# Fewer TensorE instructions ahead of W1, and the work behind W1 put in a new order

## The chip, the cores and the metric

The kernel runs on one core of one Trainium2 chip. The metric is the device time of one execution in microseconds (us). Every kernel is compared with the kernel before in alternating rounds on the same chip.

The engines are named as in the profile: PE is TensorE's matmuls, PEld its weight loads, DVE is VectorE, ACT is ScalarE, POOL is GpSimd. A query of the profile gives lines of the form "start us, busy us, engine, source line, operation, output<-inputs, shapes, xcount", and at the end in brackets how long the engine had been idle and what released it. L-numbers are lines of the kernel at hand, so the same line of code can have another number in another version. x0, x1 and x2 are the tokens of blocks 0, 1 and 2. A warm-up is a matmul on zeros whose result nobody uses. "W1 stage" stands for what begins when the first half of the weight W1 has landed.

## The reference

Eight blocks of tokens `x` (8 heads, 512 tokens, 64 wide) attend to a small state of 32 rows and the state attends to the tokens. The result goes through a max-of-two feed-forward layer.

```python
scores = scale * x @ state^T;  a = softmax(scores);   xread = a @ state
scores2 = scale * state @ x^T; a2 = softmax(scores2); sread = a2 @ x
y = concat([xread, sread])              # per block 512 + 32 rows, 8*64 = 512 wide
out = max(y @ w1, y @ w2) @ w_out       # w1, w2: 512x1024, w_out: 1024x512
```

The kernel writes max(h1, h2) as h2 + relu(h1-h2). It therefore needs W1-W2, and the product W2·Wo, which it computes once at the start. It multiplies the small states with these matrices first ("sw") and then only multiplies by the softmax weights.

## The kernel before

The parts that matter are the order of the loads, the subtraction, the state read and the program of the first block.

```python
# loads, all in one queue, in this order
load_states(first); load_x(0, 2)
for ch in range(2):
    load_w(w2f, moe_w2, ch); load_wo(2 * ch); load_wo(2 * ch + 1)
load_w(w1f, moe_w1, 0, 2)      # first half of W1, in two pieces
load_w(w1f, moe_w1, 1)         # second half of W1
load_x(1); load_states(second); load_x(2)

def states(bs):                # transpose states on TensorE, two copies on VectorE
    ...
def w_sub(q, eng=nc.gpsimd):   # a quarter of W1 - W2
    eng.tensor_sub(wcat[:, :, cs], w1f[:, :, cs], w2f[:, :, cs])
def u_sr(b):                   # state read: 32 small matmuls, then two steps on VectorE
    ...
def l1(b, fill, fs):           # per f: two matmuls, then a relu on ScalarE or VectorE
    ...

# block 0 (cut)
w_t(0, 0, "A"); w_t(0, 1, "A")          # W2's first half transposed
u_sr(0)
...
for i in range(4): w_wo(0, i)           # W2·Wo, quarter 0
u_at(0, "V"); w_cast(w2b, w2f, 1)
for i in range(4): w_wo(1, i)
w_t(1, 0, "V"); w_t(1, 1, "A")          # W2's second half transposed
negate_states(); wo_cast(2, "P"); wo_cast(3, "P"); u_srt(0); warm_up(2)
for i in range(4): w_wo(2, i)
...                                     # W1's first half cast to bf16
for i in range(4): w_wo(3, i)
...
u_sw(0, 0); u_sw(0, 2); w_sub(0); w_sub(1)
l1(0, {}, range(0, 4))
w_sub(2, nc.vector); w_sub(3, nc.vector)
compact_x(1, 0); compact_x(1, 1); d_xt(1)   # x1 cast, then transposed by a DMA
...
l2_add(0, 0, range(0, 4)); l2_add(0, 1, range(0, 4))
states(second)
l2_add(0, 2, range(0, 4)); u_sw(0, 1); l2_add(0, 3, range(0, 4))
l1(0, {}, range(4, 8))
u_sw(1, 0)
u_exp(1, 0); u_exp(1, 1)                # block 1's scores
```

The softmax here doesn't subtract the row's maximum and nothing guards it: scores larger than these inputs give would overflow.

## Time and profile before

| | before |
|---|---|
| time, median of 6 runs | 149.94 us (149.54 to 150.0, and one stray run at 186.29, which the median counts and no comparison uses) |
| span of the profiled run | 147.9 us |
| PE busy | 139.4 us, 94% |
| W1 stage starts (first product with W1) | 22.25 us |
| first product that needs W1's second half | 30.53 us |
| layer 1 of block 1 starts | 40.01 us |

TensorE is busy 94% of the span. Of the 8.5 us of idle time, 3.4 lie in the first 22 us, where the DMA engines are full, and as much after 120 us, in the tail.

One moment serves as a yardstick: the start of layer 1 of block 1. In the kernel before and in the changed kernel the span ends 107.9 us after it, so whatever a version wins or loses is won or lost by then.

```profile
40.01 2.33 PE L308 MATMUL ps<-aT,swt 128*128 128x512 bf16 x10
```

### The profile page before, as it was taken

What the parts mean: (1) busy time and instruction counts of PE and PEld (TensorE: products, weight loads), DVE (VectorE), ACT (ScalarE), POOL (GpSimd) and SP (SyncE); (2) the same over time, 40 slices, a digit from 0 to 9 for tenths busy, and PEclk for the clock granted to TensorE, in tenths of its full rate; (3) what the DMA queues carried; (4) which work ended last, traced back from release to release, by engine and by line L of the source; (5) the groups of instructions that cost most, each with busy time, mean ns of one, the idle gap of its engine ahead of it and who ended that gap; (6) DMA issues with size and microseconds to landing.
All of it is one profiled execution on the core that took longest, in us unless ns stands there. A gap on an engine that the chain in (4) does not pass through costs nothing.

```text
span 147.9 us, 3003 instructions
## 1 busy us (share of the span) xinstructions
PE 139.4 (94%) x1228; PEld 67.4 (46%) x1249; DVE 81.7 (55%) x150; ACT 75.7 (51%) x127; POOL 44.2 (30%) x48
## 2 busy tenths in 40 slices
PE   6979899999999999999999999999999999999991
PEld 2445433434454345434443454454445434764460
DVE  5448728758887187545836581668067635721130
ACT  3175538577576268446834691477167036521011
POOL 3144269551967310640072037004100500000000
PEclk9999999999999999999999999999999999999999
DMA  4999999879999939793979497760556031502423
GB/s 75 379 387 387 387 385 340 269 138 231 262 230 307 303 68 297 273 195 118 285 226 178 177 280 188 139 284 2 106 111 284 0 75 58 226 0 70 141 89 131
DMA packets 37982, 29.89 MB, mean 202 GB/s; under 512 B 24912, under 2 KB 33360, under 8 KB 37072
## 3 DMA queue, kind: packets, MB, share of 16 engines
q1 hardware_dynamic: 37824, 29.56, 69.6%
q8 instruction: 10, 0.16, 0.4%
q10 hardware_dynamic: 144, 0.13, 0.3%
q14 instruction: 4, 0.03, 0.1%
HBM read 15.20 MB, written 8.91 MB: 163 GB/s over the span
## 4 chain that ended last, share of the span: by engine, by line
PE 74%; DMA 14%; SPq 7%; ACT 2%; issue 1%
PE acc L323 34%; PE ps L308 16%; DMA xf<-in_x_dram 11%; PE acc L319 8%; SPq L97 4%; DMA xt<-xc 3%; PE ps L280 3%; PE ps L216 2%; PE ps L367 2%; PE acc L377 2%; PE ps L239 2%; SPq L100 2%; PE acc L357 1%; ACT xc L61 1%; PE acc L375 1%
## 5 line engine op out<-in xcount | busy, mean ns | idle before, releaser
L323 PE MATMUL acc<-wo,r 128*128 128x512 bf16 x238 | 58.3, 379 | 0.5
L323 PEld LDWEIGHTS <-r 128*128 128x128 bf16 x248 | 23.9, 98 | 28.3 <-issue 0.2
L298 DVE TENSOR_SCALAR r<-ps 128x512 bf16<-128x512 f32 x32 | 22.1, 692 | 13.6 <-PE ps L308 13.6
L226 POOL TENSOR_TENSOR a<-e,er 128x512 bf16<-128x512 bf16 x14 | 14.4, 1049 | 50.5 <-ACT e L219 29.6
L308 PE MATMUL ps<-aT,swt 128*128 128x512 bf16 x127 | 29.1, 379 | 0.3 <-DVE swt L63 0.2
L63 DVE COPY ob<-acc 128x512 f32<-128x512 f32 (+1 forms) x17 | 11.0, 655 | 30.2 <-PE acc L323 29.8
L61 ACT COPY ob<-acc 128x512 f32<-128x512 f32 (+1 forms) x16 | 9.2, 573 | 28.9 <-PE acc L323 13.1
L296 ACT ACTIVATE r<-ps 128x512 bf16<-128x512 f32 x32 | 19.2, 600 | 5.8 <-PE ps L308 5.2
L308 PEld LDWEIGHTS <-swt 128*128 128x128 bf16 x128 | 12.0, 98 | 15.0 <-DVE swt L63 0.8
L319 PE MATMUL acc<-swt,aT 128*128 128x512 bf16 x56 | 16.7, 380 | 0.9 <-issue 0.8
L61 ACT CAST swt<-ps 128x512 bf16<-128x512 f32 x18 | 10.0, 588 | 13.0 <-PE ps L280 13.0
L65 POOL CAST xp<-xf 128x2048 bf16<-128x2048 f32 (+1 forms) x7 | 12.2, 1745 | 11.0 <-DMA xf<-in_x_dram 11.0
L61 ACT CAST xc<-xf 128x1024 bf16<-128x1024 f32 x12 | 11.9, 1051 | 1.6 <-DMA xf<-in_x_dram 1.6
L223 DVE TENSOR_REDUCE es<-e 128x16 f32<-128x512 bf16 x16 | 10.6, 660 | 3.6 <-ACT e L219 3.6
L63 DVE CAST swt<-ps 128x512 bf16<-128x512 f32 x18 | 11.6, 678 | 1.1 <-PE ps L280 1.1
L219 ACT ACTIVATE e<-ps 128x512 bf16<-128x512 f32 x16 | 8.8, 596 | 0.8
L131 PE MATMUL ps<-warm 128*128 128x512 bf16 x24 | 7.7, 444 | 1.3 <-POOL warm L117 1.3
L412 PE MATMUL acc<-wo,w2t 128*128 128x512 bf16 x30 | 7.3, 379 | 0.8 <-POOL wo L65 0.7
L319 PEld LDWEIGHTS <-aT 128*128 128x128 bf16 x62 | 4.7, 98 | 5.9 <-issue 2.5
L280 PE MATMUL ps<-wcat,sbd 64*32 64x512 bf16 x136 | 6.2, 383 | 0.1
L216 PEld LDWEIGHTS <-xt 128*128 128x128 bf16 x128 | 4.8, 98 | 2.8 <-ACT xt L61 0.8
L216 PE MATMUL ps<-sbd,xt 128*128 128x64 bf16 x128 | 5.3, 193 | 0.7 <-ACT xt L61 0.6
(74 smaller groups left out, 118.2 us busy)
## 6 DMA issues: line engine op xcount, KB each, us to landing
xf<-in_x_dram SPq DMA_DIRECT2D x7, 1024.0 KB, 7.6
out_dram<-ob SPq DMA_DIRECT2D x7, 1024.0 KB, 5.0
w2f<-in_moe_w_dram SPq DMA_DIRECT2D x2, 1024.0 KB, 8.9
wof<-in_moe_w_out_dram SPq DMA_DIRECT2D x4, 512.0 KB, 10.8
xf<-in_x_dram SPq DMA_DIRECT2D x2, 512.0 KB, 4.4
w1f<-in_moe_w_dram SPq DMA_DIRECT2D x2, 512.0 KB, 13.5
w1f<-in_moe_w_dram SPq DMA_DIRECT2D x1, 1024.0 KB, 14.4
out_dram<-ob SPq DMA_DIRECT2D x3, 256.0 KB, 2.2
```

The source lines that it names most:

```text
L61: nc.scalar.copy(o, i)
L63: nc.vector.tensor_copy(o, i)
L65: nc.gpsimd.tensor_copy(o, i)
L216: nc.tensor.matmul(p[:, k * 64:k * 64 + 64], d["xt"][:, 4 * i + 2 * g + cp, :], sbd[:, b, 2 * i + g].rearrange("p u n -> p (u n)"), start= ...
L223: nc.vector.tensor_reduce(d["es"][:, g], d["e"][:, g].rearrange("p i c n -> p (i c) n"), axis=mybir.AxisListType.X, op=ALU.add)
L226: mul.tensor_mul(d["a"][:, g].rearrange("p c i n -> p i c n"), d["e"][:, g], d["er"][:, g].rearrange("p (i c) -> p i c", i=4).unsqueeze(3) ...
L280: nc.tensor.matmul(pg[g][32 * i:32 * i + 32, :], sneg[gs, i, :] if k else sbd[gs, b, 2 * i + g, g, :], w[gs, i, ch * 512:(ch + 1) * 512], ...
L296: nc.scalar.activation(out=o, in_=p, func=ACTF.Relu)
L298: nc.vector.tensor_scalar(o, p, scalar1=0.0, scalar2=None, op0=ALU.max)
L308: nc.tensor.matmul(p, SW[b][:, g, f * 128:(f + 1) * 128], AT[b][:, g, :], start=(g == 0), stop=(g == 1))
L319: nc.tensor.matmul(OB[b][1 + c], AT[b][:, g, c * 128:(c + 1) * 128], SW[b][:, g, FF:WC], start=(g == 0), stop=False)
L323: nc.tensor.matmul(OB[b][1 + c], R[b][:, f, c * 128:(c + 1) * 128], wo[:, f, :], start=False, stop=(f == NF - 1))
```

## The change

The intent is to have fewer TensorE instructions ahead of W1 and to bring the input of block 1 forward. x0 is transposed in 128-wide pieces (16 instructions in place of 32) and there are 13 warm-ups in place of 25. The state read of block 0 moves behind W1, and the cast of x0 that it needs moves to about 18 us, on ScalarE. W2's second half is transposed in the middle of the Wo products of quarter 1. x1 and the states are loaded ahead of W1's second half, and the order behind W1 is new.

```diff
     load_w(w1f, moe_w1, 0, 2)
-    load_w(w1f, moe_w1, 1)
     load_x(1)
     load_states(second)
+    load_w(w1f, moe_w1, 1)
     load_x(2)
 ...
-            for c in range(NC):
-                k = 2 * i + c // 2
-                nc.tensor.transpose(p[64 * (c % 2):..., ...], d["xp"][:, 2 * i + g, c, 0:64], ident)
+            for cp in range(2):
+                k = 2 * i + cp
+                nc.tensor.transpose(p[:, k * 128:(k + 1) * 128], d["xc"][:, 2 * i + g, cp * 128:(cp + 1) * 128], ident)
 ...
-    warm_up(6)
+    warm_up(3)
 ...                                   # warm_up(2), (2), (3), (1), (2) become one warm_up(1)
-    w_cast(w2b, w2f, 0, "PA")
+    w_cast(w2b, w2f, 0, "PV")
 ...
-    u_sr(0)
     wo_cast(0, "P")
     wo_cast(1, "P")
 ...
-    for i in range(4):
-        w_wo(1, i)
+    w_wo(1, 0)
+    w_wo(1, 1)
     w_t(1, 0, "V")
     w_t(1, 1, "A")
+    w_wo(1, 2)
+    w_wo(1, 3)
 ...
     l1(0, {}, range(0, 4))
-    w_sub(2, nc.vector)
-    w_sub(3, nc.vector)
 ...                                   # x1 and its states as before; x2's cast goes further down
     for c in range(NC):
         l2_open(0, c)
+    states(second)
+    u_sr(0)
+    w_sub(2, nc.vector)
+    w_sub(3, nc.vector)
     l2_add(0, 0, range(0, 4))
     l2_add(0, 1, range(0, 4))
-    states(second)
 ...
     l2_add(0, 3, range(0, 4))
-    l1(0, {}, range(4, 8))
     u_sw(1, 0)
-    u_exp(1, 0)
-    u_exp(1, 1)
+    l1(0, {5: [lambda: u_exp(1, 0), lambda: u_exp(1, 1)]}, range(4, 8))
+    u_srt(0)
```

More of the change, by code (lines that the diff above doesn't have):

```diff
@@ L180, in cast_x, with compact_x @@
             copy(e, xp[:, hs, :, 0:64], xf_t[b][:, hs].rearrange("p h (c d) -> p h c d", c=NC))
-    def compact_x(b, g, eng="A"):
+    def compact_x(b, parts=(("A", slice(0, 4)), ("A", slice(4, 8)))):
         new_x(b)
-        if g == 0:
-            st[b]["xc"] = at.tile([128, H, NC * D], BF16, tag="xc", name="xc")
-        copy(eng, st[b]["xc"][:, 4 * g:4 * g + 4], xf_t[b][:, 4 * g:4 * g + 4])
+        xc = st[b]["xc"] = at.tile([128, H, NC * D], BF16, tag="xc", name="xc")
+        for e, hs in parts:
+            copy(e, xc[:, hs], xf_t[b][:, hs])
     def d_xt(b):
@@ L195, in u_xt @@
         for i in range(4):
-            for c in range(NC):
-                k = 2 * i + c // 2
-                nc.tensor.transpose(p[64 * (c % 2):64 * (c % 2) + 64, k * 128:(k + 1) * 128], d["xp"][:, 2 * i + g, c, 0:64], ident)
+            for cp in range(2):
+                k = 2 * i + cp
+                nc.tensor.transpose(p[:, k * 128:(k + 1) * 128], d["xc"][:, 2 * i + g, cp * 128:(cp + 1) * 128], ident)
         copy(eng, d["xt"].rearrange("p (i g u) t -> p g i (u t)", g=2, u=2)[:, g], p.rearrange("p (i w) -> p i w", i=4))
@@ L428, in fillers @@
         if n + 1 < B:
-            put(8, lambda: compact_x(n + 1, 0), lambda: compact_x(n + 1, 1))
+            put(8, lambda: compact_x(n + 1))
         if n < B:
@@ L444 @@
     warm_up(9)
-    cast_x(0, (("A", slice(0, 4, 2)), ("V", slice(4, 8, 2)), ("P", slice(1, 4, 2)), ("V", slice(5, 8, 2))))
+    negate_states()
+    compact_x(0, (("A", slice(0, 4, 2)), ("V", slice(4, 8, 2)), ("P", slice(1, 4, 2)), ("V", slice(5, 8, 2))))
     u_xt(0, 0, "V")
-    warm_up(2)
     u_xt(0, 1, "A")
     u_exp(0, 0)
-    warm_up(2)
     u_exp(0, 1)
-    warm_up(3)
-    w_cast(w2b, w2f, 0, "PA")
+    warm_up(1)
+    w_cast(w2b, w2f, 0, "PV")
     u_norm(0, 0, nc.vector)
@@ L457 @@
     w_t(0, 1, "A")
-    u_sr(0)
     wo_cast(0, "P")
     wo_cast(1, "P")
-    warm_up(1)
     for i in range(4):
         w_wo(0, i)
+    w_cast(w2b, w2f, 1)
     u_at(0, "V")
-    w_cast(w2b, w2f, 1)
-    for i in range(4):
-        w_wo(1, i)
+    w_wo(1, 0)
+    w_wo(1, 1)
     w_t(1, 0, "V")
     w_t(1, 1, "A")
-    negate_states()
+    w_wo(1, 2)
+    w_wo(1, 3)
+    cast_x(0, (("A", slice(0, 4)),))
+    copy("A", st[0]["xp"][:, 4:8, :, 0:64], xf_t[0][:, 4:8].rearrange("p h (c d) -> p h c d", c=NC))
     wo_cast(2, "P")
     wo_cast(3, "P")
-    u_srt(0)
-    warm_up(2)
     for i in range(4):
@@ L487 @@
     l1(0, {}, range(0, 4))
-    w_sub(2, nc.vector)
-    w_sub(3, nc.vector)
-    compact_x(1, 0)
-    compact_x(1, 1)
+    compact_x(1)
     d_xt(1)
@@ L495 @@
     cast_states("P", second)
-    compact_x(2, 0, "P")
-    compact_x(2, 1, "P")
+    for c in range(NC):
+        l2_open(0, c)
+    states(second)
+    u_sr(0)
+    w_sub(2, nc.vector)
+    w_sub(3, nc.vector)
+    l2_add(0, 0, range(0, 4))
+    l2_add(0, 1, range(0, 4))
+    compact_x(2, (("P", slice(0, 4)), ("P", slice(4, 8))))
     d_xt(2)
     load_x(3)
-    for c in range(NC):
-        l2_open(0, c)
-    l2_add(0, 0, range(0, 4))
-    l2_add(0, 1, range(0, 4))
-    states(second)
     l2_add(0, 2, range(0, 4))
```

## The prediction

> **What bounds the kernel now.** I read, in this order, the busy shares of the page, the busy time of each engine by stretches, the timelines of the engines over the first 42 us, and the DMA packets. The stretches first (us, then busy us and instructions of each engine):
>
> ```profile
> 12.00:18.00 6.00, 5.93 (x76) 3.52 (x77) 4.42 (x10) 2.68 (x4) 1.52 (x2) 1.00 1.05 387
> 18.00:22.25 4.25, 3.49 (x16) 1.46 (x16) 1.50 (x4) 1.95 (x5) 2.87 (x4) 1.00 1.05 385
> 22.25:30.00 7.75, 7.33 (x54) 3.20 (x55) 6.08 (x9) 5.68 (x10) 5.65 (x4) 1.00 0.95 290
> 30.00:40.00 10.00, 9.77 (x118) 4.22 (x118) 7.27 (x16) 6.74 (x12) 5.67 (x7) 1.00 0.99 207
> ```
>
> Up to 22.25 the DMA engines are full (share 1.05, 385 GB/s). From 22.25 on TensorE is: it idles 0.42 us of 7.75, then 0.23 of 10, and about the same small share to the tail. So a TensorE instruction costs nothing if it runs before 22.25 beside the loads, and its full length after. What starts the second regime is this (TensorE; then ScalarE, whose cast of the first half of W1 opens it):
>
> ```profile
> 17.39 0.59 PE L131 MATMUL ps<-warm 128*128 128x512 bf16 x2
> 18.71 3.61 PE L412 MATMUL acc<-wo,w2t 128*128 128x512 bf16 x15 [0.72 <-POOL wo L65]
> 22.25 0.45 PE L280 MATMUL ps<-w1b,sbd 64*32 64x512 bf16 x8
> 23.92 1.90 PE L308 MATMUL ps<-aT,swt 128*128 128x512 bf16 x8 [0.21 <-DVE swt L63]
> ...
> 20.28 0.62 ACT L61 CAST w1b<-w1f 128x512 bf16<-128x512 f32 x1 [1.56 <-DMA w1f<-in_moe_w_dram]
> 21.64 0.62 ACT L61 CAST w1b<-w1f 128x512 bf16<-128x512 f32 x1 [0.74 <-DMA w1f<-in_moe_w_dram]
> ```
>
> Two things end together. W1's first half lands at 21.64 and is cast by 21.64+0.62 = 22.26. The last eight W2·Wo products wait for Wo: quarter 2 lands at 17.61, GpSimd casts it by 18.65, and 16 matmuls at 0.216 us (spacing in the timeline) end at 18.65+3.46 = 22.1. Both come from one load queue. TensorE work taken out ahead of 18.65 therefore gains nothing by itself: TensorE stood 0.72 us idle there even with two warm-ups before it.
>
> There is a second path by which instructions ahead of W1 could count. The page's DMA part has
>
> ```profile
> q8 instruction: 10, 0.16, 0.4%
> ```
>
> These ten packets are 16 KB each, so 256 instructions each, and ten of them are 2560, near the 1228+1255 TensorE records: they are TensorE's own program being fetched. The packet records have the first at 15.11 us, taking 1.12 us on one of the 16 engines. The 4-byte packets that end each transfer show the effect: for Wo's quarter 2 fifteen engines have ended by 15.58, the sixteenth at 17.08; for W1's first half fifteen by 19.60, the sixteenth at 21.14. One engine runs 1.5 us late from there on, and everything waits for it. Without that fetch W1's first half would be there at 21.64-1.5 = 20.1.
>
> **What the Trainium skill says.** "Perfetto Trace Analysis", The 4-stage abstract model: instructions are 64 bytes. 16 KB/64 = 256 agrees with the later fetches, which come every 256 or so recorded instructions (1206, 1462, 1718 executed). "DMA: Bandwidth & Descriptors", Why a DMA increments its semaphore by 16 and not by 1: only all 16 engines together mean that data has landed; the late sixteenth packet above agrees. "TensorE: Matmul & The Clock Gate", Part 1: a cold array runs at half clock until about 3.4 us of activity, and an idle window sends it back. The trace agrees on the first half: 0.43 us between the first matmuls, 0.22 after 4 us.
>
> ```profile
> 1.31 2.74 PE L131 MATMUL ps<-warm 128*128 128x512 bf16 x6 [1.31 <-POOL warm L117]
> 4.06 2.14 PE L131 MATMUL ps<-warm 128*128 128x512 bf16 x9
> ```
>
> "SBUF — State Buffer", Who interferes with whom: a VectorE instruction with two SBUF inputs blocks GpSimd's reads. The trace agrees: the 512-element cast of the states took 1.13 us beside VectorE's W1-W2, the 1280-element one 1.25 us without it.
>
> ```profile
> 26.46 2.35 DVE L386 TENSOR_TENSOR wcat<-w1f,w2f 128x1024 bf16<-128x1024 f32 x2
> 28.16 1.13 POOL L65 CAST s_bf<-s_f 128x512 bf16<-128x512 f32 x1 [1.39 <-DMA s_f<-in_state_dram]
> 38.36 1.25 POOL L65 CAST s_bf<-s_f 128x1280 bf16<-128x1280 f32 x1
> ```
>
> **The change part by part.** Ahead of W1, TensorE loses 16 of 32 x0 transposes (0.6 us), 12 of 25 warm-ups (9 warm at 0.22, 3 cold at 0.43: 3.3 us) and the state read of block 0 (32 small matmuls, 0.37 us). All of it lay beside the loads: gain 0. It also leaves 2 x (16+12+32) = 120 fewer TensorE instructions before W1, with weight loads counted. Transposing W2's second half between the Wo products of quarter 1 ends that work near 17 us instead of 18; the next products still wait for Wo.
>
> The fetch: [...]the regular later fetches fit a request when 256k-62 instructions have run. For the first that is 194, reached at 12.05, served at 15.11: some 3 us behind data already in that engine's queue. In the new order instruction 194 lies at the end of W2's second transposes, which need W2's second half (14.75+1.04 of cast): about 16.3. Plus 2.7 to 3 us is 19.0 to 19.3. The last W1 packets of that engine go until 19.6. So by this working the fetch still hits the second piece of W1's first half, but misses it if it is 0.4 us later. Wo, however, is freed from it: the products end near 20.7.
>
> After W1: the state read (0.37) and its transpose (0.05) now cost, +0.42. The state transposes of blocks 1 and 2 no longer wait 0.2 in the middle: their cast now runs near 26.7, before VectorE blocks it (about 0.6 instead of 1.13), so it is ready at 27.35 against TensorE's 27.4: -0.2. W1's second half is now loaded after x1 and the states; its landing moves from 24.5 to about where the states landed before, 28.1 (same bytes ahead). VectorE's W1-W2 then stands behind the states' copies (0.86) and the state read's two steps (0.45): with the old start at 22.25 those end at 29.2, the two subtractions (2.35) at 31.55. TensorE reaches the product that needs them at 27.4+0.24+0.37+12 x 0.216 = 30.6 and stalls 1.0. That product starts at 31.6 instead of 30.53: +1.07, which holds the +0.42 and -0.2 above. From it to the first L323 after the second half of layer 1 took 34.91-30.53 = 4.38 before:
>
> ```profile
> 30.53 0.41 PE L280 MATMUL ps<-wcat,sbd 64*32 64x512 bf16 x8
> 31.76 1.92 PE L308 MATMUL ps<-aT,swt 128*128 128x512 bf16 x8
> 34.14 0.71 PE L216 MATMUL ps<-sbd,xt 128*128 128x64 bf16 x16
> 34.91 0.81 PE L323 MATMUL acc<-wo,r 128*128 128x512 bf16 x3
> ```
>
> With block 1's scores put inside layer 1 and x1 transposed earlier, the waits there go: 0.34+0.86+0.34+1.73+0.47+0.06 = 3.8, and some 0.15 for activations that now have less to hide behind: -0.4. Sum if the fetch hits W1: about +0.65.
>
> If the fetch misses W1, the stage starts at 20.1+0.62 = 20.75, 1.5 earlier. But the subtractions cannot start before W1's second half, about 27.7, so the product starts at 30.1 to 30.3 and not 1.5 earlier than in the other case: -0.3 against before, then -0.5, less up to 0.9 if block 1's transposed x is not there by 32.6 (its transfer queues behind x2's load, whose packets end near 29 to 30). Sum: about -0.35.
>
> **Rivals.** (a) Fetch out of the way, as above: for it, the purpose that the cut in instructions plainly serves, and that 19.3 against 19.6 is near; against it, W1's late second half takes most back. 149.6. (b) Fetch still in W1: for it, my count; 150.55. (c) The array cools: between 6 and 13 us it would be busy some 40% where it was some 65%. For it, the removed warm-ups; against it, that Wo leaves over 1 us of slack before 18.65[...]. If it stays cold into the last 16 products, +1.7 to +3.4: 152 to 153. (d) All hidden, within noise: 149.9.
>
> **Range and chances.** I give (a) 0.45, (b) 0.42, (c) 0.08, the rest to (d). 0.45 x (-0.35) + 0.42 x 0.65 + 0.08 x 2.5 is +0.3 as a mean, +0.2 as a middle: 150.1. The range takes in (a) with all its luck and (b) with 0.8 of unforeseen waits: 149.1 to 151.4. Two per cent is 3.0 us: only (c) reaches it, and no gain I can find does. Faster 0.01, within 0.95, slower 0.04.
>
> **What would show it.** The first 16 KB packet after 18.5 us instead of 15.1; Wo quarter 2 cast from about 16.1 (17.61 before); ScalarE's second W1 cast at 20.1 in (a), 21.6 in (b); TensorE idle 1 us or so ahead of the block-0 product that needs W1's second half, released by VectorE's copy chain, and that product near 30.2 (a) or 31.6 (b); matmul spacing still 0.22 from 12 us on. I am wrong if TensorE is idle before W1 for another reason, if W1's second half lands clearly before 27 us, or if the first 22 us move by over 2 us.

## More of the kernel before

The part of the page on the chain that ended last says what the end was waiting for, by engine:

```profile
PE 74%; DMA 14%; SPq 7%; ACT 2%; issue 1%
```

By line, the DMA share holds the loads of x (11%) and x's transpose (3%), and 1% of ScalarE's 2% is the cast of x ahead of that transpose. VectorE isn't in the line at all.

## The result, and the profile after

The changed kernel takes 150.85 us (median of 6 runs, 150.71 to 150.93). The ratio to the kernel before is 1.0068, with a 95% interval of 1.0054 to 1.0082. A ratio is the mean time of one kernel's fast runs over the mean of the other's in the same rounds, so it isn't quite the ratio of the medians quoted. The change costs about 1.0 us and doesn't reach two per cent. All outputs are right.

The stretches of the profile first, as in the prediction (us of the stretch, then busy us and instructions of PE, PEld, DVE, ACT and POOL, then the granted clock, the DMA share and GB/s):

```profile
12.00:18.00 6.00, 5.34 (x45) 3.04 (x43) 4.07 (x7) 3.71 (x5) 2.93 (x5) 1.00 1.05 387
18.00:22.25 4.25, 3.60 (x20) 1.38 (x18) 0.47 (x2) 2.88 (x5) 1.65 (x3) 1.00 1.07 365
22.25:30.00 7.75, 7.44 (x81) 3.39 (x81) 5.71 (x11) 7.15 (x11) 5.09 (x4) 1.00 1.07 314
30.00:40.00 10.00, 9.28 (x116) 4.00 (x115) 7.08 (x14) 4.71 (x10) 5.01 (x5) 1.00 0.86 191
```

Up to 22.25 us the DMA engines are as full as before, and TensorE has more idle time (0.66 of 6 us, where it had 0.07). The loss is in the last line: between 30 and 40 us TensorE idles 0.72 us, where it idled 0.23.

The front on TensorE:

```profile
16.79 4.48 PE L412 MATMUL acc<-wo,w2t 128*128 128x512 bf16 x20
21.20 0.40 PE L280 MATMUL ps<-w1b,sbd 64*32 64x512 bf16 x4
22.26 0.58 PE L280 MATMUL ps<-w1b,sbd 64*32 64x512 bf16 x4 [0.66 <-DVE w1b L63]
```

The Wo products now end at 21.1 us, about 1 us sooner than before. TensorE runs the four W1 products whose data is there and then stands still until 22.26, because the second piece of W1's first half landed no sooner. ScalarE's cast of it, which waits for nothing else, began at 21.64 before and begins at 21.78 now, as the ScalarE timeline shows:

```profile
21.78 0.62 ACT L61 CAST w1b<-w1f 128x512 bf16<-128x512 f32 x1 [1.36 <-DMA w1f<-in_moe_w_dram]
```

The program fetch, a 16 KB packet, now comes at 19.45 us in the packet records (15.11 before). The last packet of that piece ends at 21.21 on one engine, where the other fifteen had ended by 19.74. The 1.5 us lag is still there. It also stays in what is loaded later: of the sixteen parts of W1's second half, fifteen have landed by 26.52 us and the last lands at 28.10.

Behind W1 (TensorE):

```profile
27.84 0.44 PE L239 MATMUL ps<-xp,e 128*32 128x65 bf16 x32
...
31.65 0.41 PE L280 MATMUL ps<-wcat,sbd 64*32 64x512 bf16 x8 [0.68 <-DVE wcat L386]
...
35.60 1.28 PE L323 MATMUL acc<-wo,r 128*128 128x512 bf16 x4
...
41.18 1.04 PE L308 MATMUL ps<-aT,swt 128*128 128x512 bf16 x4
```

The first line is the state read in its new place. The second is the product that needs W1's second half. It starts at 31.65 in place of 30.53 and has waited for VectorE. The last is the yardstick: 41.18 in place of 40.01, so 1.17 us are lost by then. The VectorE timeline shows what the product waited for:

```profile
27.94 0.86 DVE L63 COPY sbd<-ps 64x512 bf16<-64x512 bf16 x2 [1.26 <-PE ps L155]
...
29.25 2.35 DVE L386 TENSOR_TENSOR wcat<-w1f,w2f 128x1024 bf16<-128x1024 f32 x2
```

VectorE was idle 1.26 us, then copied the states, did the state read's two steps, and only then subtracted. W1's second half had landed at 28.10, in the middle of the copies. The subtraction ends at 31.60 and the product follows. The chain of the page names VectorE now:

```profile
PE 79%; DMA 9%; SPq 5%; DVE 4%; issue 1%; ACT 0%
```

On GpSimd, the cast of the states behaves as predicted. It runs before VectorE takes up its two-input subtraction, and takes 0.62 us where it took 1.13:

```profile
26.73 0.62 POOL L65 CAST s_bf<-s_f 128x512 bf16<-128x512 f32 x1
```

A detail was easy to misread. TensorE's four products at 35.60 waited for their relu. The first line is the weight loads of those four products before, the others are the last two of the four after:

```profile
34.66 0.56 PEld L323 LDWEIGHTS <-r 128*128 128x128 bf16 x4
```

```profile
36.23 0.10 PEld L323 LDWEIGHTS <-r 128*128 128x128 bf16 x1 [0.53 <-ACT r L296]
36.49 0.10 PEld L323 LDWEIGHTS <-r 128*128 128x128 bf16 x1 [0.17 <-DVE r L298]
```

Before there are four weight loads from 34.66 on. The matmul view, quoted in the prediction, has only three matmuls, from 34.91. One matmul record is missing there. With a spacing of 0.22 us the four products began at about 34.69 and not at 34.91. They took 0.96 us (34.69 to the next group at 35.65). After, they take 1.22 (35.60 to 36.82).

### The profile page after: what moved, and what is told of

The parts are those of the page before. It is cut to its first block, busy times and chain, and to the rows that moved or that the text cites. A ratio compares the mean times of both kernels' runs of the same rounds, so it can differ in the third digit from the quotient of the medians.

```text
span 149.1 us, 2971 instructions
## 1 busy us (share of the span) xinstructions
PE 139.1 (93%) x1221; PEld 66.6 (45%) x1221; DVE 81.8 (55%) x151; ACT 76.5 (51%) x128; POOL 44.3 (30%) x48
## 4 chain that ended last, share of the span: by engine, by line
PE 79%; DMA 9%; SPq 5%; DVE 4%; issue 1%; ACT 0%
PE acc L323 34%; PE ps L308 19%; PE acc L319 10%; DMA w1f<-in_moe_w_dram 9%; PE ps L280 3%; SPq L97 3%; PE ps L367 2%; PE acc L377 2%; PE ps L216 2%; PE ps L239 2%; SPq L100 2%; DVE wcat L386 2%; PE acc L357 1%; PE acc L375 1%; PE acc L280 1%; DVE wcat L63 1%
## 5 line engine op out<-in xcount | busy, mean ns | idle before, releaser
L323 PE MATMUL acc<-wo,r 128*128 128x512 bf16 x248 | 59.1, 379 | 0.0
L323 PEld LDWEIGHTS <-r 128*128 128x128 bf16 x248 | 23.9, 98 | 28.9 <-ACT r L296 0.5
L319 PE MATMUL acc<-swt,aT 128*128 128x512 bf16 x62 | 18.1, 381 | 0.0
L61 ACT CAST xc<-xf 128x1024 bf16<-128x1024 f32 (+1 forms) x13 | 12.6, 1017 | 3.2 <-DMA xf<-in_x_dram 3.2
L65 POOL CAST xp<-xf 128x2048 bf16<-128x2048 f32 x6 | 11.3, 1889 | 9.3 <-DMA xf<-in_x_dram 9.3
L131 PE MATMUL ps<-warm 128*128 128x512 bf16 x13 | 4.9, 524 | 1.3 <-POOL warm L117 1.3
```

What stands on the lines that cost most here:

```text
L61: nc.scalar.copy(o, i)
L65: nc.gpsimd.tensor_copy(o, i)
L319: nc.tensor.matmul(OB[b][1 + c], AT[b][:, g, c * 128:(c + 1) * 128], SW[b][:, g, FF:WC], start=(g == 0), stop=False)
L323: nc.tensor.matmul(OB[b][1 + c], R[b][:, f, c * 128:(c + 1) * 128], wo[:, f, :], start=False, stop=(f == NF - 1))
```

## The experiments

Theory: the front is worth nothing, and the loss lies behind W1. It consists of the state read on the path, the order of VectorE's work (states and state read ahead of the subtractions), and the activations of layer 1 having less time with block 1's scores between them. Rivals: the thin front itself costs (the array cools, or the fetch hits something), or W1's late second half does.

The kernel before had a median of 149.76 us. All experiments had five timed rounds. Each has six runs, r4_at_late has four.

### Behind W1: r8_back_only

The kernel before, with its old front and without the early state read, but with the new load order and the new order behind W1.

```diff
+    load_w(w1f, moe_w1, 1)         # moved behind load_states(second)
 ...
-    u_sr(0)                        # ahead of wo_cast(0)
 ...
+    states(second)                 # behind l2_open
+    u_sr(0)
+    w_sub(2, nc.vector)
+    w_sub(3, nc.vector)
 ...
-    u_exp(1, 0); u_exp(1, 1)
+    l1(0, {5: [lambda: u_exp(1, 0), lambda: u_exp(1, 1)]}, range(4, 8))
```

> Edit to the kernel before: only the part of the change behind W1 (x1 and the states loaded ahead of W1's second half, states transposed early, state read of block 0 behind W1, the subtractions behind the states' copies, block 1's scores inside layer 1); the front with its warm-ups stays. Theory 'order behind W1': the whole loss is here: 150.7 to 151.0, the product on W1's second half at about 31.6, released by VectorE's subtraction, as in the changed kernel. Rival 'the front loses (cold array, casts)': the back alone is within 0.2 us of the kernel before: 149.7 to 150.0.

Measured: 151.03 us (150.75 to 151.32), ratio 1.008 (1.0064 to 1.0096). The product waits as in the changed kernel, and the yardstick is at 41.34:

```profile
31.81 0.41 PE L280 MATMUL ps<-wcat,sbd 64*32 64x512 bf16 x8 [0.68 <-DVE wcat L386]
```

The whole loss is there with the old front. It lies behind W1.

### The late state read alone: r9_sr_late

The kernel before, with only the state read and its transpose moved behind W1.

```diff
-    u_sr(0)                        # ahead of wo_cast(0)
 ...
-    u_srt(0)
 ...
     l2_add(0, 1, range(0, 4))
+    u_sr(0)
     states(second)
 ...
     l1(0, {}, range(4, 8))
+    u_srt(0)
```

> Edit to the kernel before: only the state read of block 0 and its transpose go behind W1 (between the layer-2 products of block 0, ahead of the states' transposes, and behind layer 1). Theory: +0.42 us of TensorE work on the path, less 0.2 us that TensorE stood waiting for the states there: 149.95 to 150.2. Rival 'instruction count ahead of W1 matters': 66 fewer instructions ahead of W1 shift the program fetch and save over 0.3 us: below 149.5.

Measured: 150.05 us (149.85 to 150.43), ratio 1.0017 (1.0002 to 1.0032): +0.26 us. The yardstick moved by 0.27:

```profile
29.58 0.40 PE L155 MATMUL ps<-ident,s_bf 128*128 128x128 bf16 x4
...
40.28 1.90 PE L308 MATMUL ps<-aT,swt 128*128 128x512 bf16 x8
```

The state transposes follow the state read without a wait (before they waited for their cast). So the 0.37 us of state read and 0.05 of its transpose cost only about 0.26: part of the read fills a wait that was there.

### The subtractions first: r7_back_sub_first

r8_back_only, with two pairs of lines exchanged.

```diff
-    states(second)
-    u_sr(0)
     w_sub(2, nc.vector)
     w_sub(3, nc.vector)
+    states(second)
+    u_sr(0)
```

> Edit to the back-only kernel: VectorE's two W1-W2 subtractions go ahead of the states' copies and of the state read's two steps. Theory 'order on VectorE': the product on W1's second half starts at 30.9 (TensorE's own arrival) instead of 31.6, 0.7 us less than the back-only run. Rival 'taken back by block 1': TensorE then waits for x1's transpose, whose landing the program fetch or the load queue sets (32.7 in the changed kernel), and the gain is under 0.2 us.

Measured: 150.19 us (149.76 to 150.37), ratio 1.0016 (0.9999 to 1.0033), 0.84 us less than r8_back_only in the same rounds. VectorE:

```profile
28.00 2.36 DVE L386 TENSOR_TENSOR wcat<-w1f,w2f 128x1024 bf16<-128x1024 f32 x2 [1.43 <-DMA w1f<-in_moe_w_dram]
```

TensorE:

```profile
30.78 0.41 PE L280 MATMUL ps<-wcat,sbd 64*32 64x512 bf16 x8
```

The subtraction starts when its data lands, and the product no longer waits: 30.78 in place of 31.81. The yardstick is at 40.43. This order of four lines is most of the loss.

### The scores behind layer 1: r11_scores_after

r7_back_sub_first, with block 1's scores put behind the second half of layer 1, as they were before.

```diff
-    l1(0, {5: [lambda: u_exp(1, 0), lambda: u_exp(1, 1)]}, range(4, 8))
+    l1(0, {}, range(4, 8))
+    u_exp(1, 0)
+    u_exp(1, 1)
```

> The run of the back part with the subtractions first (150.19), with block 1's scores moved from inside the second half of layer 1 to behind it, as in the kernel before. Theory (the activations of layer 1 and of the scores, ScalarE and VectorE, are what the four products after layer 1 wait for): the 0.36 us of waits in those products (1.22 instead of 0.86) go, layer 1 of block 1 starts at 40.0 to 40.15 instead of 40.43, time 149.75 to 149.95. Rival (the waits only move, to the scores' transposed output or to the normalisation that layer 1 of block 1 needs): start at 40.4, time 150.1 to 150.3.

Measured: 149.80 us (149.62 to 150.07), ratio 1.0007 (0.9992 to 1.0022). TensorE in r7_back_sub_first, then here:

```profile
34.85 1.28 PE L323 MATMUL acc<-wo,r 128*128 128x512 bf16 x4
```

```profile
34.76 1.03 PE L323 MATMUL acc<-wo,r 128*128 128x512 bf16 x4
...
40.08 2.12 PE L308 MATMUL ps<-aT,swt 128*128 128x512 bf16 x9
```

The four products take 0.96 us again (34.76 to 35.72) in place of 1.22, and the yardstick moved from 40.43 to 40.08. The 0.35 us are these 0.26 and 0.09 of a sooner start. The two versions ran in different calls and their intervals overlap, so the size rests on the two profiles.

### Without the late read: r10_no_late_read

r11_scores_after, with the state read where the kernel before has it, ahead of W1. Of the change this version keeps the load order and the earlier states and x1.

```diff
     w_t(0, 1, "A")
+    u_sr(0)
     wo_cast(0, "P")
 ...
     states(second)
-    u_sr(0)
```

> The kernel before with only the new order of loads and the new order behind W1, but with the subtractions first on VectorE, the scores behind layer 1, and the state read left where the kernel before has it, ahead of W1. Theory (what the new order of loads and work gained was eaten by the late state read, by VectorE's order and by the activation waits): layer 1 of block 1 starts at 39.6 to 39.8 (40.01 before), time 149.35 to 149.65. Rival (the new order of loads has nothing to give, the product is held by W1's second half which lands at 28.0): product at 30.5 as before, start at 40.0, time 149.7 to 149.95.

Measured: 149.24 us (149.11 to 149.66), ratio 0.9972 (0.9956 to 0.9988), a little better than the range of the theory. This version beats both kernels, by 0.5 and 1.6 us in the medians (the latter from different rounds).

```profile
39.85 2.33 PE L308 MATMUL ps<-aT,swt 128*128 128x512 bf16 x10
```

The profiled run was one of the slow ones (149.57), so its 39.85 understates the gain over 40.01. Against r11_scores_after, in the same rounds, the median is 0.56 us lower, though the profiles differ by only 0.23. The new load order does have something to give: in the kernel before (first line), the scores' weight loads waited for x1's transpose, and here (second line) that wait is gone.

```profile
34.14 0.59 PEld L216 LDWEIGHTS <-xt 128*128 128x128 bf16 x16 [0.42 <-DMA xt<-xc]
```

```profile
33.85 0.72 PEld L216 LDWEIGHTS <-xt 128*128 128x128 bf16 x16
```

How much of the 0.5 us is this wait and how much the wait for the states' cast (0.56 us on the weight loads before, 0.20 here), isn't shown.

### The warm-ups put back: r5_more_pe

The changed kernel with 11 of the 12 warm-ups back.

```diff
-    warm_up(3)
+    warm_up(6)
 ...                               # and warm_up(2), (2), (3) for (1), warm_up(2) in quarter 1
```

> Edit to the changed kernel: eleven of the twelve removed warm-ups come back (22 more TensorE instructions ahead of W1). Theory 'beside the loads': nothing before W1 is bound by TensorE, the fetch comes earlier (about 18.7) but W1's first half still lands at 21.7: 150.7 to 151.0, no change. Rival 'TensorE ahead of W1 counts': 11 matmuls at 0.22 to 0.43 us are 2.4 to 4 us of TensorE, of which at least 1 us shows: over 151.8.

Measured: 150.86 us (150.55 to 151.28), ratio 1.0075 (1.0063 to 1.0087). The changed kernel has 150.85. The fetch came at 18.41 us in place of 19.45 and still fell into W1's first half. So 22 more instructions, with weight loads counted, cost nothing, and leaving them out gains nothing.

### The front alone: r6_front_only

The kernel before with the changed front; the state read goes right behind the Wo products of quarter 2, and its transpose stays behind layer 1.

```diff
-    warm_up(6)
+    warm_up(3)
 ...                               # the whole front of the change
     for i in range(4):
         w_wo(2, i)
+    u_sr(0)
```

> Edit to the kernel before: the part of the change ahead of W1 alone (wide transposes, fewer warm-ups, W2's second half transposed amid the Wo products, state read of block 0 late but still ahead of W1); load order and everything behind W1 as before. Theory: the fetch still hits W1 (at about 19.4), W1's first half at 21.7, so the front is worth nothing: 149.7 to 150.1, the same as before. Rival 'the front gains, the back loses': 149.0 to 149.4, over 0.5 us faster than before.

Measured: a median of 150.69 us, a miss. The six runs are 149.78 and 149.82 (as the kernel before), 150.24 and 151.14, all at full clock, and 151.21 and 151.84 at a mean clock of 0.986 and 0.989. The profiled run is the slowest. The windows show why (the clock is the third number from the end):

```profile
12.00:15.00 3.00, 2.38 (x10) 0.96 (x9) 2.24 (x5) 1.81 (x3) 1.52 (x3) 0.50 1.05 386
```

The array ran at half clock from 11.80 to 15.21 us, 3.41 us in all. This used up the slack ahead of W1, into which this version had also put the state read. VectorE's two steps of that read then stood ahead of its cast of W1, which took 2.40 us beside GpSimd's subtraction (0.43 in the changed kernel), and TensorE waited 0.75 us for it. No long idle time precedes the stretch at half clock: from 6 to 12 us TensorE is busy 3.08 of 6 us and its longest idle time is 1.06 us. In the kernel before it is busy 4.78 of these 6 us. The two runs at full clock that were slow weren't traced, so their cause is open.

### Both repairs at once: r3_both

The changed kernel with the state read right behind the Wo products of quarter 2 and the subtractions first.

```diff
     for i in range(4):
         w_wo(2, i)
+    u_sr(0)
 ...
-    states(second)
-    u_sr(0)
     w_sub(2, nc.vector)
     w_sub(3, nc.vector)
+    states(second)
```

> Edit to the changed kernel: block 0's state read goes back ahead of W1 (after the Wo products of quarter 2), and VectorE's two W1-W2 subtractions go ahead of the states' copies. Theory 'order behind W1': VectorE's subtractions start when W1's second half has landed (28.07) and end at 30.45, TensorE reaches the product that needs them at about 30.5 instead of 30.9, so the product starts at 30.6 and not 31.65; time 149.8 (-1.0 to -1.1 against the changed kernel's 150.85). Rival 'late load': the late landing of W1's second half itself is the loss; then the product still starts above 31.3 and the time stays above 150.5. Rival 'cooler or slower front': nothing moves, 150.85.

Measured: 150.92 us (150.80 to 152.75), ratio 1.0088 (1.0067 to 1.011), a miss. The profiled run is the one at 152.75, with half clock from 11.99 to 15.40. VectorE and GpSimd in it:

```profile
22.03 2.33 DVE L63 CAST w1b<-w1f 128x512 bf16<-128x512 f32 x1
```

```profile
21.73 4.85 POOL L386 TENSOR_TENSOR wcat<-w1f,w2f 128x1024 bf16<-128x1024 f32 x2 [2.20 <-DMA w1f<-in_moe_w_dram]
```

VectorE's cast of a piece of W1 takes 2.33 us, where it takes 0.43 in the changed kernel. The state read's two steps stood ahead of it, so it started 0.30 us after GpSimd's subtraction, and ended about when the first half of that did. "SBUF — State Buffer", Who interferes with whom, in the Trainium skill, says that whichever of the two issues first has the shared port pair for its whole instruction. The trace agrees. Later TensorE waited 0.80 us for x1's transpose.

Four of the other runs took 150.8 to 150.9 at full clock, and a fifth 151.94 at 0.998. None was traced, so why they gained nothing is open. A candidate is the second program fetch. In r12_front_and_fixes below, it comes at 31.94 us and the last of sixteen pieces of x1's transpose lands at 34.07, 1.6 us behind the others. That is harmless with the scores behind layer 1 (they start at 34.13), but it would cost about 1 us with them inside layer 1, where r3_both has them. This is argued, not shown.

### A later fetch: r4_at_late

The changed kernel with one warm-up less and eight transposes moved behind the Wo products of quarter 1, so that the fetch should miss W1.

```diff
-    warm_up(1)
 ...
-    u_at(0, "V")
     w_wo(1, 0)
     w_wo(1, 1)
+    w_wo(1, 2)
     w_t(1, 0, "V")
     w_t(1, 1, "A")
-    w_wo(1, 2)
     w_wo(1, 3)
+    u_at(0, "V")
```

> Edit to the changed kernel: the last warm-up ahead of W2's first transposes goes, and block 0's eight transposes of the attention go from ahead of the Wo products of quarter 1 to behind them, so that TensorE's 194th instruction comes some 0.6 us later. Theory 'program fetch': the first 16 KB packet is served after 19.9 us (19.45 before), behind the last piece of W1's first half; ScalarE's second W1 cast then starts at 20.3 to 20.6 instead of 21.78, the first W1 products are complete from 21.2 on instead of 22.26, and the product on W1's second half starts at 30.4 (bound by its landing) instead of 31.65: 149.6 to 149.8. Rival 'bandwidth': W1's first half comes at 21.7 whatever TensorE's program does: 150.8, or more if the moved transposes get in the way.

Measured: 151.18 us (151.06 to 151.33), ratio 1.0096 (1.0083 to 1.0109), a miss. The fetch came at 19.69, not after 19.9, and W1's first half was as late as ever. VectorE's cast of its second piece waits only for that data, and began at 21.92 (21.78 in the changed kernel):

```profile
21.92 0.43 DVE L63 CAST w1b<-w1f 128x512 bf16<-128x512 f32 x1 [1.69 <-DMA w1f<-in_moe_w_dram]
```

Besides, all four runs had a mean clock of 0.985 to 0.989, and the profiled one was at half clock from 13.28 to 16.69. With that TensorE reached the W1 products only at 22.88. What a fetch that misses W1 is worth stays unmeasured.

### The change with two repairs: r12_front_and_fixes

The changed kernel, front and late state read included, with only the edits of r7_back_sub_first and r11_scores_after.

```diff
-    states(second)
-    u_sr(0)
     w_sub(2, nc.vector)
     w_sub(3, nc.vector)
+    states(second)
+    u_sr(0)
 ...
-    l1(0, {5: [lambda: u_exp(1, 0), lambda: u_exp(1, 1)]}, range(4, 8))
+    l1(0, {}, range(4, 8))
+    u_exp(1, 0)
+    u_exp(1, 1)
```

> The changed kernel with only the two repairs that worked behind the old front: the two subtractions first on VectorE, and block 1's scores behind layer 1. Theory (the new front is worth nothing and costs nothing in an undisturbed run, all of the loss is VectorE's order, the activation waits and the late state read): as with the old front, layer 1 of block 1 starts at 40.0 to 40.2, time 149.7 to 150.0 in runs with an undisturbed clock, and 151 to 152 in runs with a half-clock stretch near 12 to 15 us if that stretch makes the work ahead of W1 late. Rival (the new front itself costs something behind W1, as the run that moved the state read ahead of W1 and put the subtractions first suggests, which stayed at 150.8 to 150.9 in undisturbed runs): 150.5 to 150.9, with TensorE waiting for x1's transpose (its landing after 34 us) or for the second subtraction.

Measured: 149.78 us (149.68 to 150.19), ratio 1.0008 (0.9988 to 1.0028). With the old front it was 149.80 (r11_scores_after). So these two edits take back the whole loss, and the front is worth nothing either way. Three of the six runs had a mean clock of 0.988 (149.68, 149.77, 150.13), three had the full clock (149.72, 149.79, 150.19), and their times don't differ. The profiled run is one of the former. Its windows and its TensorE:

```profile
12.00:15.00 3.00, 2.75 (x15) 1.41 (x13) 2.21 (x5) 1.97 (x3) 1.53 (x3) 0.56 1.05 386
```

```profile
17.86 4.48 PE L412 MATMUL acc<-wo,w2t 128*128 128x512 bf16 x20
22.27 0.41 PE L280 MATMUL ps<-w1b,sbd 64*32 64x512 bf16 x8
```

The Wo products start 1.07 us later than in the changed kernel's profile (17.86 and 16.79). They end at about 22.2, just when W1 has been cast. The half clock ate exactly the slack that the thin front had made. In r6_front_only and r3_both the state read and its wait stood in the same gap, and there was nothing left.

### A version of my own: n1_open_first and n2_x2_early

The changed kernel with nine of the twelve warm-ups back, Wo's products by row block so that they are copied out early, layer 2 of block 0 opened ahead of layer 1, and the state read in the wait for W1. n1_open_first also loads x2 late, so as to keep it away from x1's transpose; n2_x2_early undoes that.

```diff
# n1_open_first, against the changed kernel (core)
-    load_x(2)                      # up front
+    w_wo(2, 0); w_wo(2, 1); w_wo(3, 0); w_wo(3, 1)   # then copies, then rows 2 and 3
+    u_sr(0)
+    u_sw(0, 2)
+    u_sw(0, 0)
+    for c in range(NC): l2_open(0, c)
+    l1(0, {1: [lambda: cast_states("A", second)]}, range(0, 4))
 ...
+    load_x(2)                      # behind d_xt(1); compact_x(2), d_xt(2) behind u_norm(1)
# n2_x2_early, against n1_open_first
+    load_x(2)                      # up front again
+    compact_x(2, ...); d_xt(2)     # behind the subtractions again
```

> A version meant to beat both, on the changed kernel: the removed warm-ups are back; the Wo products are finished one row block after the other and copied out as they end, so that the layer-2 openings of block 0, which need W2.Wo but not W1, run while W1's first half is being cast; the state read of block 0 stands in TensorE's wait for W1; VectorE casts nothing of W1 there (GpSimd does, ahead of its subtraction); block 1's scores follow layer 1. From its parts: openings end near 25 instead of 27.5, layer 1 near 26.6, the product on W1's second half near 30.5 (landing 28.1 plus 2.35 of subtraction), first layer-2 product with the second half of layer 1 near 34 against 34.9 in the kernel before and 35.6 in the changed one: 148.8 to 149.3. If W1's first half or x1's transpose is later than that, 149.8 to 150.5.

Measured: 153.89 us (153.15 to 154.41), ratio 1.0266, a miss.

```profile
46.20 0.64 PE L215 MATMUL ps<-sbd,xt 128*128 128x64 bf16 x16 [2.50 <-DMA xt<-xc]
```

x2's cast on GpSimd ended at 40.4 us and its transpose was issued then. Block 1 needed it at 43.7.

> The version that opened layer 2 first and failed by its late load of x2 (153.89), with x2's load, compaction and transpose put back to where the changed kernel has them. Theory (the 2.50 us wait for x2's transposed tile was the whole loss, the front's 0.4 to 0.9 us is real): layer 1 of block 1 starts at 39.7 to 40.1, no wait for xt in block 1, time 149.0 to 149.8. Rival (x2's load in front of x1's transpose costs block 1 its scores' input): a wait on xt(1) near 33 to 36 us, time 150.3 to 151.5.

Measured: 149.51 us (149.45 to 149.91), ratio 0.9993 (0.9976 to 1.0011). The wait is gone, and 4.4 us of the median with it; the yardstick is at 39.76 us (40.07 in n1_open_first). The wait itself was 2.50 us. In the profile of n1_open_first the array then ran at half clock from 47.13 to 50.55 us, which is an estimated 1.7 us more (half of 3.41). Two runs of n1_open_first had the full clock and still took 153.15 and 153.45; they weren't traced. The new front doesn't separate from the kernel before, and r10_no_late_read is better.

## Why the prediction was right or wrong

The prediction was right in its class and in its range: 150.85 lies between 149.1 and 151.4, and the difference is under two per cent. The predicted 150.1 is a mean of two cases. The case that came true, (b), had been put at 150.55. So the point of 150.1 was 0.75 us low, and it is the width of the range that holds the result. The class was safe from the start, since two per cent are 3 us.

**The front is worth 0.** Right. r5_more_pe and r12_front_and_fixes show it: 150.86 and 150.85 with and without the warm-ups, 149.78 and 149.80 with the new and the old front.

**The fetch.** Predicted at 19.0 to 19.3 and still in W1's first half; seen at 19.45 and still there. Wo, freed from it, was cast from 16.22 (predicted 16.1). The Wo products ended at 21.1 (20.7 predicted), which was useless, since the W1 cast began at 21.78. The working behind 19.0 to 19.3, some 3 us after TensorE's 194th instruction, was right by luck. That instruction lies in W2's second transposes, which run from 15.90 us on in the changed kernel and from 16.97 on in r12_front_and_fixes, and the fetch came at 19.45 and 19.42. In r4_at_late it lies in the attention's transposes, from 18.88 on, and the fetch came at 19.69. Case (a), which I had given a little more weight, didn't occur in any traced run, so its value of 149.6 is untested.

**The late state read, +0.42, and the states, -0.2.** r9_sr_late measured the two together: +0.26. With the rest of the order mended, the late read cost 0.56 us in the medians (r11_scores_after against r10_no_late_read), which is more than its 0.42 us of TensorE work; why isn't shown.

**VectorE's order.** Predicted: the subtractions end at 31.55 and the product starts at 31.6, after a stall of 1.0. Seen: 31.60 and 31.65, after a stall of some 0.85 (the twelve products from 28.21 on leave TensorE free at 28.21 + 12 x 0.216 = 30.80). r7_back_sub_first shows that the order and not the landing of W1 causes it: 0.84 us came back by exchanging two pairs of lines. I had the number and put it down as a cost of the change. I didn't see that the cost wasn't tied to it.

**From the product to the next L323, -0.4.** This is the step that failed, as a size. The interval after was predicted as 3.8 + 0.15 and is 3.95 (31.65 to 35.60). But the 4.38 of before was misread: a matmul record is missing, and the group began at about 34.69, so it was 4.16. The gain is 0.21. And the wait for activations doesn't end at that point: the four products took 1.22 us in place of 0.96. In all: +1.12 for the product, -0.21, +0.26 gives +1.17, which is the yardstick's 41.18-40.01. I had +0.65. r11_scores_after shows the activation term by itself (0.35 us).

**Rival (c), the array cools.** I gave it 0.08 and put it at 152 to 153. The busy share between 6 and 13 us fell from 82% to 52% (5.73 and 3.64 of 7 us), where I had written 65% and 40%. The cooling was far more frequent: three of six runs of the changed kernel had a mean clock of 0.985 to 0.987. It comes with the missing warm-ups. Of the 28 runs of the five versions with the thin front, 13 had a mean clock of 0.989 or less; of the 42 runs of the seven with all or most of the warm-ups, none did, though r5_more_pe and n2_x2_early among them keep the rest of the thin front (n1_open_first is left out, whose half clock came after its wait for x2). That the untraced runs had their stretch near 12 us too is inferred from those that were traced. But the three cooled runs of the changed kernel took 150.71 to 150.82, and the three at full clock 150.89 to 150.93. The slack of over 1 us that I named as an argument against it did absorb it (r12_front_and_fixes). Where the slack was used for the state read (r6_front_only, r3_both), the profiled half-clock runs took 151.84 and 152.75.

## What to carry to other kernels

When a load is put behind others, look at which instructions stand on the engine that will use it, and let that one run as soon as the data lands. Here four lines of VectorE's order were 0.84 of a 1 us loss, and the same loads gave a gain of 0.5 us once that order was mended, the scores stood behind layer 1 and the state read was back ahead of W1. Work removed beside a load-bound stretch gains nothing but slack, and that slack may be what pays for a drop of the clock. Count weight loads beside matmuls before you take an interval from a profile, since one missing record was worth 0.22 us here.

## What the Trainium skill lacked or had wrong

- "Runtime: NRT & Kernel Launch", Instruction fetch mechanics, has the fetch in blocks of 16 KiB and its cost "mostly hidden". It lacks that a fetch can delay a load on the path: the 16 KB packet takes 1.12 us on one of the 16 DMA engines, and with the queues full that engine ends W1's first half 1.5 us behind the others (21.21 and 19.74 us in the changed kernel).
- "TensorE: Matmul & The Clock Gate", Part 1, has half clock after an idle window of about 3.4 us, and windows that run free of the kernel. It lacks how busy a window must be. Here a stretch of 3.41 us at half clock came after 3.41 us in which TensorE was busy 1.46 us (r4_at_late), 1.48 (r6_front_only), 1.57 (r3_both) and 1.89 (r12_front_and_fixes), with no idle time over 1.28 us in them. After 1.69 us in the profiled run of the changed kernel and 2.08 in r5_more_pe the clock stayed full, so this share alone doesn't decide it.
